# Where the later heads' values live, when they are loaded, and when the attention's output is written out

## The chip, the core and the metric

The kernel runs on one core of one Trainium2 chip. The metric is the device time of one execution in microseconds. Times of the kernel before are the median of three runs; the profile is one further execution, recorded by the hardware profiler.

## What is computed

Attention over 4 batches of 8 heads, with 32 global and 512 local positions of width 64 and a window of 32; its output is a matrix of 2176 rows and 512 columns, which goes through two MLPs without biases:

```python
out_g = np.matmul(sm(s_g), v_all)                 # global queries see every key
s_ll = np.where(mask, s_ll, -1000000000.0)        # local ones a window and the global keys
out_l = np.matmul(sm(np.concatenate([s_lg, s_ll], -1)), v_all)
x = np.concatenate([out_g, out_l], axis=2).transpose(0, 2, 1, 3).reshape(B * S, H * D)
h = np.maximum(x @ moe_w_in, 0.0)                 # d_ff 2048
x = h * h @ moe_w_out
h = (x @ moe2_w1) * (x @ moe2_w2) @ moe2_w3       # d_ff 1024
return h @ moe2_w_out
```

## The kernel before

Everything is float32 at the interface. Matrices of the MLPs, and keys, queries and values of the later heads, are split into a high and a low part that TensorE takes at full rate, and products are made of three passes (high by high, high by low, low by high).

The first part of the program, up to about 345 us, mixes attention with the first half of MLP 1. The loop `for i in range(0, NBLK, 2)` takes two blocks of rows (one batch's output, 256 and 288 columns) through the MLP in each turn. Its `main` list holds their matmul steps (`h_unit` with the weights ua, `x_unit_a` with ub); `merge` lays between them the attention `steps` of the next batch, b = i/2 + 1. So turn 0 carries batch 1, turn 2 batch 2 and turn 4 batch 3; turn 6 has no attention left and carries the conversions of further weights (`conv(16)` to `conv(32)`) instead. The steps come from `cycle(j)`: for a pair of heads, `emit_k` splits the keys and queries of the next pair (DVE L173 and L106) and moves them by five transfers per head (L179 to L183) into kq_hl; `emit_g` makes the global scores sg and pg (ACT L267, DVE L271 to L273), for which POOL copies global queries into qgp (L237); `emit_s` makes the local scores sc and softmax p (DVE L200, ACT L204, DVE L208 and L209, POOL L214); `emit_tg` and `emit_t` transpose pg and p into pt (tg L293, tp L305); `emit_pv` multiplies with the values and copies the result to xb (ACT L342, DVE L345 to L349).

Heads 0 to 15 use values in float32 (v_f). From head 16 (`FIRST_SPLIT`) on, `load_v` (L157) loads vraw and `emit_v` splits it into v_hl: a cast on DVE (L163) and a subtraction on POOL (L106); it then asks for the values two heads on. pt of these heads is a pair too, pt_hl.

Conversions take a weight matrix from DRAM (`load_w`, L409, into wraw) and turn it into a high and a low part: ACT L415 and L416, DVE L421 and L424, POOL L434, ACT L435, DVE L106.

Memory on chip is dealt out by pools that open and close like a stack on two sides. `cv` holds the conversions' buffers, `at` those of attention. At turn 2 both close, and `at2` (vraw and v_hl) and `sp` (pt_hl) take their places; at turn 6 the attention's pools close and `cv2` and `u2` open. What a new pool's tile lies on must have been read for the last time. `spill(i)` (L565) writes the attention's output of block i to DRAM (x_d), from where MLP 2's part fetches it again (`load_x`, L600); xb has two buffers, one for each batch in flight.

Each engine runs its instructions in one fixed order. That order is made when the program is built, by a scheduler that starts from the order of the code and moves instructions past each other. All transfers are issued from one queue, SP's, in its order.

Of the kernel before, what the change touches and what calls it, by code (L numbers as in the profile page):

```python
# [9 lines left out]
F32 = mybir.dt.float32  # L10
F32R = mybir.dt.float32r
# [9 lines left out]
B, H, SL, SG, D = 4, 8, 512, 32, 64  # L21
# [46 lines left out]
FIRST_SPLIT = 16  # L68
# [7 lines left out]
def attention_mlp(ctx: ExitStack, tc: tile.TileContext, kq0, kq, vw, wts, mask, ident, out):  # L76
    nc = tc.nc
# [3 lines left out]
    def pool(name, side="left", **kw):  # L81
        return tc.tile_pool(name=name, bufs=1, side=side, reuse_waits="tile", **kw)
# [3 lines left out]
    cv_cm, rot_cm, at_cm = pool("cv"), pool("rot", "right"), pool("at", "right")  # L86
    cv, rot, at = cv_cm.__enter__(), rot_cm.__enter__(), at_cm.__enter__()
# [12 lines left out]
    x_d = dram.tile([128, 4, NT], F32, name="x_d")  # L100
# [11 lines left out]
    pools = {"ua": sb, "ub": sb, "cv": cv}  # L112
# [9 lines left out]
    pair_t, kq_raw, kq_t, v_raw, v_t, p_t, pt_t = {}, {}, {}, {}, {}, {}, {}  # L122
# [25 lines left out]
    def load_v(i, part=None):  # L148

        if i >= (H if part is not None else B * H):  # L150
            return
        if i >= FIRST_SPLIT:
            t = v_raw[i] = at.tile([128, 8, D], F32, tag="vraw", name="vraw", bufs=2)
        else:
            t = v_t[i] = at.tile([128, 8, D], F32, tag="v", name="v_f32", bufs=3)
        c = slice(0, 8) if i >= H else slice(4, 8) if part == 0 else slice(0, 6)
        nc.sync.dma_start(out=t[:, c], in_=vw[i, :, c])  # L157

    def emit_v(i):
        if i >= FIRST_SPLIT:  # L160
            raw = v_raw.pop(i)
            t = v_t[i] = at.tile([128, 2, 8, D], F32R, tag="v", name="v_hl", bufs=2)
            nc.vector.tensor_copy(t[:, 0], raw)  # L163
            split_lo(nc.gpsimd, t[:, 1], raw, t[:, 0])
            load_v(i + 2)
# [109 lines left out]
    def new_pt(i):  # L275
        if i < FIRST_SPLIT:
            pt_t[i] = at.tile([128, 8, 160], F32, tag="pt", name="pt_f32", bufs=3)
        else:
            pt_t[i] = pools["cv"].tile([128, 2, 8, 160], F32R, tag="pt", name="pt_hl", bufs=2)

    def put_pt(i, to, src):

# [240 lines left out]
    def of(t, i):  # L523
        s, n = block(i)
        return t[:, :, s : s + n]
# [33 lines left out]
    def xcols(i):  # L559
        s, n = block(i)  # L560
        s -= S * (i // 2)
        return x_t[i // 2][:, :, s : s + n]

    def spill(i):
        nc.sync.dma_start(out=of(x_d, i), in_=xcols(i))  # L565

    steps = first_part()
    merge(steps, ([lambda n=n: conv(n) for n in range(8)], 0, len(steps) - 2))
# [7 lines left out]
    steps = [f for j in range(-1, 4) for f in cycle(j, ahead=j < 3)]  # L576
    main = [lambda f=f: h_unit(0, f, f) for f in range(8)]
# [18 lines left out]
    def load_x(i):  # L596

        if i < NBLK:
            t = x_t[i] = sb.tile([128, 2, 4, NB], F32, tag="xb", name="xl", bufs=2)[..., : block(i)[1]]
            nc.sync.dma_start(out=t[:, 0], in_=of(x_d, i))  # L600
            nc.sync.dma_start(out=t[:, 1], in_=of(part_d, i))

    for i in range(0, NBLK, 2):
        main = []
        for j in (i, i + 1):
            if j >= SHARED:
                main += rows(
                    j, 0, 8, lambda d, j=j: split_a(j + 1, d), lambda d, j=j: end_a(j, d, acc[d])
                )
                continue  # L610
            if j > 0:
                main += [lambda f=f, j=j: h_unit(j, f, f) for f in range(8)]
            main += [lambda d=d, j=j: x_unit_a(j, d) for d in range(4)]
        b = i // 2 + 1
        if b < B:
            if b == 1:
                spill(1)
                load_kq(H // 2)
                for k in range(H, min(H + 3, FIRST_SPLIT)):
                    load_v(k)  # L620
            if b * H == FIRST_SPLIT:
                at_cm.__exit__(None, None, None)
                cv_cm.__exit__(None, None, None)
                at_cm, cv_cm = pool("at2", "right"), pool("sp")
                at, pools["cv"] = at_cm.__enter__(), cv_cm.__enter__()
                for k in range(2):
                    load_v(FIRST_SPLIT + k)
            steps = [s for j in range(4 * b - 1, 4 * b + 4) for s in cycle(j, j < 4 * b + 3, j >= 4 * b)]
            steps.append(lambda i=i: (spill(i + 2), spill(i + 3)))
            fills = [(steps, 0, len(main) - 5)]  # L630
        else:
            for cm in (at_cm, rot_cm, cv_cm):
                cm.__exit__(None, None, None)
            u2 = pools["va"] = pools["vb"] = ctx.enter_context(pool("u2", "right"))
            pools["cv"] = ctx.enter_context(pool("cv2"))
            load_w(16)
            load_w(17)
            main.insert(18, lambda: load_x(0))
            fills = [([lambda n=n: conv(n) for n in range(16, 33)], 0, 31)]
        merge(main, *fills)  # L640

# [30 lines left out]
    main = []  # L672
# [146 lines left out]
```

## Time and profile before

| | |
|---|---|
| median of three runs | 945.86 us (944.57 to 948.61) |
| the profiled execution | 945.08 us, its span 943.3 us |
| PE busy | 899.1 us (95%) |
| DVE, ACT, POOL busy | 469.6, 499.5, 321.2 us |
| mean granted TensorE clock | 0.989 |

Busy time says how long an engine had an instruction running. The span is what the trace covers, from the first instruction to the last; the profiled execution's own time is 1.8 us more. The granted clock is a share of full speed: 1.0 is 2.4 GHz and 0.5 is 1.2 GHz. In the lists below, "PE" is TensorE, "PEld" its weight load, "SPq" the issue of a transfer on SP's queue. What stands in brackets at the end of a row is how long the engine was idle before it, and what let it go on.

### The profile page before, as it was taken

What the parts mean: (1) busy time and instruction counts of PE and PEld (TensorE: products, weight loads), DVE (VectorE), ACT (ScalarE), POOL (GpSimd) and SP (SyncE); (2) the same over time, 40 slices, a digit from 0 to 9 for tenths busy, and PEclk for the clock granted to TensorE, in tenths of its full rate; (3) what the DMA queues carried; (4) which work ended last, traced back from release to release, by engine and by line L of the source; (5) the groups of instructions that cost most, each with busy time, mean ns of one, the idle gap of its engine ahead of it and who ended that gap; (6) DMA issues with size and microseconds to landing.
All of it is one profiled execution on the core that took longest, in us unless ns stands there. A gap on an engine that the chain in (4) does not pass through costs nothing.

```text
span 943.3 us, 16424 instructions
## 1 busy us (share of the span) xinstructions
PE 899.1 (95%) x6064; PEld 822.3 (87%) x6064; DVE 469.6 (50%) x1139; ACT 499.5 (53%) x1291; POOL 321.2 (34%) x354
## 2 busy tenths in 40 slices
PE   7899899799999999988999999999999999999998
PEld 4677798699999989987999999999988888888886
DVE  6984465466867649999354353994110210200201
ACT  6975767657667748887464464884211211211211
POOL 5593452376656824433011121430211111111111
PEclk9999999989999999999999999999999999999999
DMA  8644667665668335656144333654200110100101
GB/s 269 204 148 115 168 156 186 184 142 127 156 188 200 84 108 172 227 178 202 32 157 146 132 112 134 207 192 133 98 23 1 43 42 1 42 1 1 42 1 42
DMA packets 61952, 113.07 MB, mean 120 GB/s; under 512 B 6320, under 2 KB 37168, under 8 KB 61872
## 3 DMA queue, kind: packets, MB, share of 16 engines
q1 hardware_dynamic: 61872, 112.03, 40.3%
q8 instruction: 48, 0.79, 0.3%
q14 instruction: 32, 0.26, 0.1%
HBM read 71.63 MB, written 19.92 MB: 97 GB/s over the span
## 4 chain that ended last, share of the span: by engine, by line
PE 63%; DMA 12%; DVE 10%; ACT 4%; issue 4%; POOL 4%; SPq 3%; DVEq 0%; POOLq 0%; ACTq 0%
PE ab L110 20%; PE acc L504 16%; PE h L110 9%; PE wacc L652 5%; PE x L110 4%; DMA wraw<-in_wts 4%; PE o L339 4%; DMA kq_hl<-kqhi 3%; PE sc L110 2%; DMA kqraw<-in_kq 2%; DVE wt L421 2%; DVE wt L424 2%; PE tp L305 2%; DVE hl L106 2%; POOL wt L434 1%
## 5 line engine op out<-in xcount | busy, mean ns | idle before, releaser
L434 POOL TENSOR_TENSOR wt<-wt 128x512 int32<-128x512 int32 x72 | 101.5, 1409 | 232.8 <-DVE wt L424 158.3
L723 DVE TENSOR_TENSOR r<-r,ab 128x480 f32<-128x480 f32 (+1 forms) x40 | 24.3, 607 | 220.2 <-PE ab L110 219.5
L110 PE MATMUL h<-hl,ua 128*128 128x256 f32 (+1 forms) x768 | 121.3, 303 | 8.5 <-ACT r L470 6.1
L110 PEld LDWEIGHTS h<-hl,ua 128*128 128x128 f32 x768 | 107.7, 200 | 12.4 <-ACT r L470 7.0
L504 PE MATMUL acc<-hl,vb 128*128 128x256 f32 (+1 forms) x768 | 112.9, 290 | 5.2 <-DVE hl L106 4.9
L110 PE MATMUL h<-hl,va 128*128 128x256 f32 (+1 forms) x768 | 112.3, 288 | 1.9 <-DVE hl L106 1.9
L106 POOL TENSOR_TENSOR hl_c<-r,hl_c 128x480 fp32r<-128x480 f32 x32 | 39.2, 1224 | 210.8 <-ACT hl_c L725 203.0
L504 PEld LDWEIGHTS acc<-hl,vb 128*128 128x128 f32 x768 | 103.0, 188 | 9.0 <-DVE hl L106 7.3
L110 PEld LDWEIGHTS h<-hl,va 128*128 128x128 f32 x768 | 102.9, 188 | 3.7 <-DVE hl L106 2.8
L110 PE MATMUL x<-hl,ub 128*128 128x288 f32 (+1 forms) x576 | 88.8, 295 | 3.3 <-POOL hl L106 3.3
L504 PE MATMUL acc<-hl_c,wv 128*128 128x480 f32 x384 | 89.2, 380 | 0.0
L110 PE MATMUL ab<-hl_c,ua 128*128 128x480 f32 x384 | 87.1, 380 | 0.0
L110 PE MATMUL ab<-hl_c,ub 128*128 128x480 f32 x384 | 86.6, 380 | 0.0
L110 PEld LDWEIGHTS ab<-hl_c,ub 128*128 128x128 f32 x384 | 72.0, 188 | 11.9
L722 ACT COPY r<-ab 128x480 f32<-128x480 f32 (+1 forms) x40 | 20.9, 522 | 116.1 <-PE ab L110 113.8
L110 PEld LDWEIGHTS ab<-hl_c,ua 128*128 128x128 f32 x384 | 71.9, 188 | 11.9
L110 PEld LDWEIGHTS x<-hl,ub 128*128 128x128 f32 x576 | 76.8, 189 | 6.1 <-POOL hl L106 4.5
L504 PEld LDWEIGHTS acc<-hl_c,wv 128*128 128x128 f32 x384 | 72.0, 188 | 11.4
L204 ACT ACTIVATE p<-p,st 128x256 f32<-128x256 f32 x128 | 64.2, 504 | 22.5 <-DVE st L200 22.3
L214 POOL TENSOR_TENSOR p<-p,st 128x512 f32<-128x512 f32 x56 | 61.8, 1106 | 35.4 <-DVE st L209 27.6
L470 ACT ACTIVATE r<-h 128x288 f32<-128x288 f32 (+1 forms) x128 | 49.2, 391 | 43.9 <-PE h L110 43.3
L415 ACT ACTIVATE wt<-wraw 128x512 f32<-128x512 f32 x72 | 48.4, 672 | 34.9 <-DMA wraw<-in_wts 32.4
(108 smaller groups left out, 1554.7 us busy)
## 6 DMA issues: line engine op xcount, KB each, us to landing
wraw<-in_wts SPq DMA_DIRECT2D x72, 512.0 KB, 3.4
kq_hl<-kqhi SPq DMA_DIRECT2D x24, 280.0 KB, 3.2
kq_hl<-kqraw SPq DMA_DIRECT2D x48, 136.0 KB, 3.2
vraw<-in_vw SPq DMA_DIRECT2D x16, 256.0 KB, 3.3
x2l<-x_d SPq DMA_DIRECT2D x4, 960.0 KB, 6.0
out<-y SPq DMA_DIRECT2D x16, 240.0 KB, 2.3
kqraw<-in_kq SPq DMA_DIRECT2D x24, 144.0 KB, 2.9
kq_hl<-kqraw SPq DMA_DIRECT2D x24, 144.0 KB, 3.4
```

Source lines behind the costliest of these rows:

```text
L106: eng.tensor_tensor(out=lo, in0=raw, in1=hi.bitcast(F32), op=ALU.subtract)
L110: mm(o, w, x, start=(k == 0), stop=(k == len(terms) - 1))
L204: nc.scalar.activation(p[:, n, :], p[:, n, :], AF.Exp, bias=least[:, n : n + 1], scale=-1.0, accum_out=sums[:, n, 0:1],)
L214: nc.gpsimd.tensor_tensor(out=p, in0=p, in1=over.unsqueeze(2).to_broadcast([128, 2, 256]), op=ALU.mult)
L339: mm(to, w, x, start=(k == 0), stop=(k == len(terms) - 1))
L415: nc.scalar.activation(t[0].bitcast(F32), raw[:, :, 1].bitcast(F32), AF.Copy, scale=2.0**-112)
L434: nc.gpsimd.tensor_tensor(out=b, in0=b, in1=m, op=ALU.add)
L470: nc.scalar.activation(r, h, AF.Relu)
L504: mm(acc[d], w[:, a, 128 * d : 128 * (d + 1)], g_t[f][:, b], start=(f + k == 0), stop=(f + k == 9),)
L652: mm(o, w3[:, a, 128 * q : 128 * (q + 1)], w_t[32 + 4 * half + q][:, b], start=(half + q + k == 0), stop=(half + q + k == 6),)
L722: nc.scalar.copy(r, a)
L723: nc.vector.tensor_tensor(out=r, in0=r, in1=b, op=ALU.mult)
```

## The change

Four things are different. At turn 0, as soon as the first 16 conversions are done, `cv` closes and `sp` opens on its memory; vraw and v_hl of the later heads lie in `sp`. At turn 2 `at` closes and `at2` opens; it now holds pt_hl. The first two loads of split values (heads 16 and 17) move from the start of turn 2 to the middle of the attention steps of turn 1's batch, that is of turn 0. The spills of a batch's output move from the end of the batch's own steps (block 1: from the start of turn 0) to the tenth place of the MLP steps of the next turn, and they are kept in program order: the scheduler doesn't move them.

```diff
--- before.py
+++ after.py
@@ -150,7 +150,7 @@
         if i >= (H if part is not None else B * H):
             return
         if i >= FIRST_SPLIT:
-            t = v_raw[i] = at.tile([128, 8, D], F32, tag="vraw", name="vraw", bufs=2)
+            t = v_raw[i] = pools["cv"].tile([128, 8, D], F32, tag="vraw", name="vraw", bufs=2)
         else:
             t = v_t[i] = at.tile([128, 8, D], F32, tag="v", name="v_f32", bufs=3)
         c = slice(0, 8) if i >= H else slice(4, 8) if part == 0 else slice(0, 6)
@@ -159,7 +159,7 @@
     def emit_v(i):
         if i >= FIRST_SPLIT:
             raw = v_raw.pop(i)
-            t = v_t[i] = at.tile([128, 2, 8, D], F32R, tag="v", name="v_hl", bufs=2)
+            t = v_t[i] = pools["cv"].tile([128, 2, 8, D], F32R, tag="v", name="v_hl", bufs=2)
             nc.vector.tensor_copy(t[:, 0], raw)
             split_lo(nc.gpsimd, t[:, 1], raw, t[:, 0])
             load_v(i + 2)
@@ -276,7 +276,7 @@
         if i < FIRST_SPLIT:
             pt_t[i] = at.tile([128, 8, 160], F32, tag="pt", name="pt_f32", bufs=3)
         else:
-            pt_t[i] = pools["cv"].tile([128, 2, 8, 160], F32R, tag="pt", name="pt_hl", bufs=2)
+            pt_t[i] = at.tile([128, 2, 8, 160], F32R, tag="pt", name="pt_hl", bufs=2)
 
     def put_pt(i, to, src):
 
@@ -562,7 +562,7 @@
         return x_t[i // 2][:, :, s : s + n]
 
     def spill(i):
-        nc.sync.dma_start(out=of(x_d, i), in_=xcols(i))
+        tc.keep_in_program_order(nc.sync.dma_start(out=of(x_d, i), in_=xcols(i)))
 
     steps = first_part()
     merge(steps, ([lambda n=n: conv(n) for n in range(8)], 0, len(steps) - 2))
@@ -614,19 +614,20 @@
         b = i // 2 + 1
         if b < B:
             if b == 1:
-                spill(1)
+                cv_cm.__exit__(None, None, None)
+                cv_cm = pool("sp")
+                pools["cv"] = cv_cm.__enter__()
                 load_kq(H // 2)
                 for k in range(H, min(H + 3, FIRST_SPLIT)):
                     load_v(k)
             if b * H == FIRST_SPLIT:
                 at_cm.__exit__(None, None, None)
-                cv_cm.__exit__(None, None, None)
-                at_cm, cv_cm = pool("at2", "right"), pool("sp")
-                at, pools["cv"] = at_cm.__enter__(), cv_cm.__enter__()
-                for k in range(2):
-                    load_v(FIRST_SPLIT + k)
+                at_cm = pool("at2", "right")
+                at = at_cm.__enter__()
             steps = [s for j in range(4 * b - 1, 4 * b + 4) for s in cycle(j, j < 4 * b + 3, j >= 4 * b)]
-            steps.append(lambda i=i: (spill(i + 2), spill(i + 3)))
+            if (b + 1) * H == FIRST_SPLIT:
+                steps.insert(len(steps) // 2, lambda: [load_v(FIRST_SPLIT + k) for k in range(2)])
+            main.insert(9, lambda i=i: spill(i + 1) if i == 0 else (spill(i), spill(i + 1)))
             fills = [(steps, 0, len(main) - 5)]
         else:
             for cm in (at_cm, rot_cm, cv_cm):
@@ -635,7 +636,8 @@
             pools["cv"] = ctx.enter_context(pool("cv2"))
             load_w(16)
             load_w(17)
-            main.insert(18, lambda: load_x(0))
+            main.insert(9, lambda i=i: (spill(i), spill(i + 1)))
+            main.insert(19, lambda: load_x(0))
             fills = [([lambda n=n: conv(n) for n in range(16, 33)], 0, 31)]
         merge(main, *fills)
```

What the scheduler makes of it is seen on three engines. The first place is SP's queue at the boundary between batch 1 and batch 2; kqraw are the raw keys and queries of pair 9, kq_hl their split parts (first five transfers: head 18). Brackets name what is waited for. Before:

```order
L146 DMA kqraw<-in_kq 64x576 [waits DMAHW3_49]
L179 DMA kq_hl<-kqhi 64x1120 [waits DVE_49,DMAHW4_49,PE_49,Pool_49]
L180 DMA kq_hl<-kqhi 64x544 [waits DMAHW5_49]
L181 DMA kq_hl<-kqraw 64x576 [waits DMAHW6_49,DMAHW0_49,DVE_49]
L565 DMA x_d<-xb 512x1x256 [waits DMAHW7_49,Activation_49]
L157 DMA vraw<-in_vw 128x512
L157 DMA vraw<-in_vw 128x512 [waits DMAHW1_49,PE_49]
L565 DMA x_d<-xb 512x1x288 [waits DMAHW2_49,DVE_49]
L182 DMA kq_hl<-kqraw 64x544 [waits DMAHW3_49]
L183 DMA kq_hl<-kqraw 64x544 [waits DMAHW4_49]
L179 DMA kq_hl<-kqhi 64x1120 [waits DMAHW5_49,PE_49,Pool_49]
```

After:

```order
L146 DMA kqraw<-in_kq 64x576 [waits DMAHW6_49]
L565 DMA x_d<-xb 512x1x288 [waits DMAHW7_49]
L179 DMA kq_hl<-kqhi 64x1120 [waits DVE_49,DMAHW0_49,PE_49,Pool_49]
L180 DMA kq_hl<-kqhi 64x544 [waits DMAHW1_49]
L181 DMA kq_hl<-kqraw 64x576 [waits DMAHW3_49,DMAHW2_49,DVE_49]
L182 DMA kq_hl<-kqraw 64x544
L183 DMA kq_hl<-kqraw 64x544 [waits DMAHW4_49]
L179 DMA kq_hl<-kqhi 64x1120 [waits DMAHW5_49,PE_49,Pool_49]
```

The spill of block 1 (512x1x288) now stands between the last load of keys and the first move; the two loads of vraw, and the spills of blocks 2 and 3 (512x1x256 and 512x1x288), no longer stand between the moves L181 and L182.

The second place is VectorE at the same boundary, in the softmax of heads 16 and 17 (st_82 to st_85) and the global scores of that pair (stg_86). Before:

```order
L163 CAST v_hl<-vraw 128x512
L208 TENSOR_REDUCE st_82<-st_82 128x2
L163 CAST v_hl<-vraw 128x512
L209 RECIPROCAL st_82<-st_82 128x2
...
L208 TENSOR_REDUCE st_83<-st_83 128x2
L209 RECIPROCAL st_83<-st_83 128x2
L271 TENSOR_REDUCE stg_86<-stg_86 64x1
L272 RECIPROCAL stg_86<-stg_86 64x1
L273 TENSOR_SCALAR pg<-pg,stg_86 64x640
```

After:

```order
L208 TENSOR_REDUCE st_82<-st_82 128x2
L209 RECIPROCAL st_82<-st_82 128x2
...
L208 TENSOR_REDUCE st_83<-st_83 128x2
L209 RECIPROCAL st_83<-st_83 128x2
L271 TENSOR_REDUCE stg_86<-stg_86 64x1
L272 RECIPROCAL stg_86<-stg_86 64x1
L273 TENSOR_SCALAR pg<-pg,stg_86 64x640
```

The two casts L163 are gone from here; they stand where L271 to L273 of pair 3's global scores are (77 us in the trace before), one cast between L271 and L272, one behind L273.

The third place is ACT at the start of turn 6, behind the last copies of the attention's output. Before:

```order
L342 COPY xb<-o 64x256
L460 CAST hl<-xb 128x256
L342 COPY xb<-o 64x256
L582 COPY st<-x 128x288
L415 ACTIVATE wt<-wraw 128x512
L416 ACTIVATE wt<-wraw 128x512
L470 ACTIVATE r<-h 128x256
L415 ACTIVATE wt<-wraw 128x512
```

After:

```order
L342 COPY xb<-o 64x256
L460 CAST hl<-xb 128x256
L342 COPY xb<-o 64x256
L415 ACTIVATE wt<-wraw 128x512
L416 ACTIVATE wt<-wraw 128x512
L582 COPY st<-x 128x288
L470 ACTIVATE r<-h 128x256
L415 ACTIVATE wt<-wraw 128x512
L416 ACTIVATE wt<-wraw 128x512
```

The first conversion, L415 and L416, now stands ahead of the copy L582 and of the relu L470. On SP the loads of these weights (L409) waited before for the last products with values, with the spill of block 6 ahead of them and that of block 7 behind; after, the first waits for POOL's split of head 31's values, and both spills stand behind five further loads.

On TensorE, 36 h matmuls follow the transposes tg of pair 8 before; after, they are followed by two matmuls of sg for the next pair, four transposes tp and 12 h matmuls. On POOL, the cast L237 that needs the last moves (L182, L183) of head 18 stands after ahead of L473 and L106 of the MLP, and before behind them.

## Rows read from the trace of the kernel before

**Rows 1.** Windows by stage: us, PE, PEld, DVE, ACT, POOL busy (x count), PEclk, DMA share, GB/s.
```profile
170.00:200.00 30.00, 22.87 (x151) 21.75 (x151) 14.18 (x46) 13.80 (x45) 16.32 (x23) 0.83 0.70 181
200.00:345.00 145.00, 143.79 (x1316) 141.44 (x1315) 101.42 (x355) 99.36 (x312) 93.44 (x118) 1.00 0.54 135
345.00:440.00 95.00, 84.31 (x636) 81.20 (x635) 84.26 (x123) 75.27 (x175) 35.83 (x26) 0.98 0.59 195
```

**Rows 2.** Waits in 170 to 200 us: us in total, times, longest.
```profile
PE tg L293 <- DVE st L208: 4.7, 1, 4.7
...
PE o L339 <- DVE xb L347: 1.9, 1, 1.9
```

**Rows 3.** Timeline of the first boundary: start us, us, engine, line, operation [idle before <-releaser].
```profile
177.64 0.21 POOL L237 CAST qgp<-kq_hl 128x32 fp32r<-128x32 f32 x1 [9.84 <-DMA kq_hl<-kqhi]
...
179.47 0.61 POOL L473 TENSOR_TENSOR r<-r 128x256 f32<-128x256 f32 x1 [1.62 <-ACT hl L471]
...
180.16 0.74 POOL L106 TENSOR_TENSOR hl<-r,hl 128x256 fp32r<-128x256 f32 x1
...
181.98 0.20 ACT L267 ACTIVATION_READ_ACCUMULATOR pg<-pg,stg 64x1 f32 x1
...
182.23 1.11 PE L110 MATMUL x<-hl,ub 128*128 128x256 f32 x8
...
183.15 0.43 DVE L163 CAST v_hl<-vraw 128x512 fp32r<-128x512 f32 x1 [2.86 <-DMA vraw<-in_vw]
...
186.13 0.13 DVE L271 TENSOR_REDUCE stg<-stg 64x1 f32<-64x3 f32 x1
...
186.49 1.40 DVE L273 TENSOR_SCALAR pg<-pg,stg 64x640 f32<-64x640 f32 x1
186.51 1.04 POOL L214 TENSOR_TENSOR p<-p,st 128x512 f32<-128x512 f32 x1
```

**Rows 4.** All of line L273: count, min/median/max ns, first and last start.
```profile
L273 DVE TENSOR_SCALAR pg<-pg,stg x16: 534/546/1402, 48.5 to 321.6; 64x640 f32<-64x640 f32 x16
```

**Rows 5.** Timeline of SP's issues at the first boundary.
```profile
173.70 0.49 SPq L179 DMA_DIRECT2D kq_hl<-kqhi  x1
...
175.72 0.65 SPq L565 DMA_DIRECT2D x_d<-xb  x1
...
176.42 2.13 SPq L157 DMA_DIRECT2D vraw<-in_vw  x2
...
179.26 0.63 SPq L182 DMA_DIRECT2D kq_hl<-kqraw  x1
```

**Rows 6.** Timeline of PE before and after the stop, same shape.
```profile
180.81 1.57 PE L110 MATMUL h<-hl,ua 128*128 128x256 f32 x12
...
188.73 7.17 PE L110 MATMUL h<-hl,ua 128*128 128x256 f32 x36
```

**Rows 7.** Windows around the stops of the first boundary, columns as in the first group.
```profile
174.10:177.60 3.50, 3.50 (x17) 3.17 (x16) 2.12 (x9) 1.12 (x3) 0.00 (x0) 0.51 0.81 159
...
187.80:194.60 6.80, 6.57 (x32) 6.48 (x33) 1.39 (x8) 1.78 (x6) 5.83 (x10) 0.50 0.55 161
```

**Rows 8.** Timeline of the second boundary.
```profile
344.83 0.36 ACT L342 COPY xb<-o 64x256 f32<-64x256 f32 x1
...
350.96 0.66 ACT L415 ACTIVATE wt<-wraw 128x512 f32<-128x512 f32 x1 [2.63 <-DMA wraw<-in_wts]
...
352.50 0.73 PE L110 MATMUL h<-hl,ua 128*128 128x256 f32 x4 [2.13 <-ACT r L470]
```

**Rows 9.** DMA issues of the whole span: count, KB each, median us from issue to landing.
```profile
wraw<-in_wts SPq DMA_DIRECT2D x72, 512.0 KB, 3.4
...
x_d<-xb SPq DMA_DIRECT2D x4, 576.0 KB, 6.1
```

**Rows 10.** Lines of DVE, 200 to 345 us: busy, mean ns, idle before.
```profile
L163 DVE CAST v_hl<-vraw 128x512 fp32r<-128x512 f32 x14 | 8.3, 593 | 2.0 <-PE o L339 1.1 <-issue 0.4 <-POOL qgp L237 0.3
```

**Rows 11.** Timeline in the first batches, POOL.
```profile
82.60 1.04 POOL L214 TENSOR_TENSOR p<-p,st 128x512 f32<-128x512 f32 x1 [4.85 <-DVE st L209]
```

## The prediction

> **What bounds the kernel now.** I read first the table of stretches [rows 1]. It shows a kernel that is TensorE almost throughout: PE is busy 143.79 of 145 us while batches 2 and 3 run. Two stretches leak. At the boundary from batch 1 to batch 2 (170 to 200 us) PE works 22.87 of 30 us and its mean clock is 0.83; in 345 to 440 us, where attention has ended and the second run of conversions starts, it works 84.31 of 95. What the change can win lies in these 7.1 and 10.7 us of idle time and in the low clock; elsewhere it can only cost.
>
> Next I read who ends the waits there. At the first boundary one wait is most of the stretch: 4.7 us in front of the transposes tg of pair 8 [rows 2]. The reader should follow it backwards in the timeline [rows 3]. PE's x matmuls end at 182.23 + 1.11 = 183.34, then comes nothing until tg. tg needs pg scaled by L273, and L273 starts only at 186.49, although ACT's last read of the sums, on which L271 to L273 depend, ends at 181.98 + 0.20 = 182.18. Between stands VectorE's own order: the cast L163 of head 16's values, which waited 2.86 us for vraw, a second cast, and the softmax sums behind them. vraw is late because its two loads were issued at 176.42 [rows 5], between other transfers: at2 and sp, which hold it, open only at this boundary.
>
> At the second boundary [rows 8] ACT's last copy of the attention ends at 344.83 + 0.36 = 345.19, and the first conversion L415 starts at 350.96, after a wait for the first weights, whose load stands on SP behind the last PV and beside the last spills. L470, which releases the next MLP chain, is behind it in ACT's order, so PE has a wait of 2.13 at 352.50.
>
> **The change, part by part.** The profiled execution took 945.08 us, its span 943.3; the sum is made against 945.08, and 945.86 (the median) is 0.78 more.
>
> *The stall before tg.* The order after has no L163 between L200 and L273 of pair 8. L271 to L273 can then follow ACT's 182.18. From L271's start to L273's are 186.49 − 186.13 = 0.36, and L273 itself has a median of 0.546 [rows 4]: 182.18 + 0.36 + 0.55 = 183.1, before PE's 183.34. So all of 4.7 can go. But L273 took 1.40 here, while POOL's L214 ran from 186.51 [rows 3]. If it meets POOL again, it ends at 182.18 + 0.36 + 1.40 = 183.94, 0.6 after PE. The bounds are −4.7 and −4.1; I take −4.4. The Trainium skill, page "SBUF — State Buffer", section "Who interferes with whom", has the rule for it: VectorE and GpSimd share one pair of ports as an exclusive lock, and a tensor_scalar in its fast mode and a GpSimd instruction can hold each other up. The rows agree (1.40 against 0.546); by the rule this term is −4.1 if POOL works at 182.5, −4.7 if it rests.
>
> *The clock.* After the stall the granted clock is 0.50 from 187.80 to 194.60 [rows 7], the lower of the two levels (1.2 GHz), and 36 h matmuls take 7.17 us, while 12 of the same shape took 1.57 just before the stall [rows 6]: 36 at that rate are 4.71. If PE doesn't stand still, 7.17 − 4.71 = 2.46 is won. Below nothing is excluded, since those matmuls can't run slower than at the lower level. Bounds −2.5 and 0; I take −2.5: the lower level follows PE's stops, here the one of 4.7 us, and in 174.10 to 177.60 (0.51) one of 1.9 us [rows 2, 7].
>
> *Spill(1) just ahead of the keys.* The order moves the 576 KB write of block 1 from batch 1's first third to a place in front of L179 at 173.70 [rows 5], and takes vraw and the spills of 2 and 3 from between L181 and L182. The second is the gain that makes room: L182 can start where the spill stood, 175.72, instead of at 179.26, so SP is 3.5 us ahead. The first costs: the write shares the engines with the loads of the next keys and with the kq_hl moves. It landed 6.1 us after its issue in the median [rows 9]; a kq_hl move landed after 177.64 − 173.70 = 3.9 [rows 3, 5]. If the moves behind the spill lose the difference, 2.2, this is the price; nothing, if they share. I take +0.6. The Trainium skill, page "DMA: Bandwidth & Descriptors", section "Issuing engines are not separate DMA queues", says that all transfers run on the same 16 engines and interleave; by it the spill isn't served whole before the next move, and the price stays below 2.2. No row isolates this.
>
> *POOL's new order.* After, the second qgp cast of head 18 stands ahead of L473 and L106 (before at 179.47 and 180.16, ending at 180.90). It needs L183, now issued about 0.65 behind 175.72, so landed at 176.4 + 3.9 = 180.3, cast by 180.5: L106 then ends near 182.0, and the x matmuls which read it run from 182.23. Zero, with 0.2 in hand; it costs the spill's 2.2 once more if that cover is gone, which is the first rival.
>
> *The values loaded early.* Two loads, two casts and two splits stand now near 70 to 82 us, one cast between L271 and L272 of an earlier pair. A cast is 0.593 [rows 10]; POOL waits 4.85 before 82.60 there [rows 11], which hides two splits, each about the price of L214 here (1.04). One cast delays tg of that pair by at most 0.6. I take +0.2 (0 to 0.9).
>
> *The other spills.* Those of blocks 2 to 5 go to the middle of the steps of batches 2 and 3, where MLP matmuls hide what keys and values wait for: PE stands idle 145 − 143.79 = 1.2 us in all there [rows 1]. Zero, and 6.1 − 3.4 = 2.7 each [rows 9] if a weight or key load had to pay for it. Those of 6 and 7 go behind five weight loads: L565 no longer shares the engines with the first two, but with later ones. +0.5 (0 to 2.7).
>
> *The start of the conversions.* The order has vraw's memory, not pt's, under the new weights: the first load waits for POOL's split of head 31 and no longer for the last PV, and L415 follows L342 directly. At best L415 starts at 345.19 instead of 350.96: −5.8. At the least PE's wait of 2.13 goes, since L470 is no longer behind a wait for a load [rows 8]. The whole stretch follows the conversions' pace, but the second L415 stays behind L470; I take the middle, −4.0.
>
> Sum: −4.4 − 2.5 + 0.6 + 0.2 + 0.5 − 4.0 = −9.6, so 935.5 for an execution like the profiled one, and 936.3 beside the median. I forecast **936.3**.
>
> **The rivals.** *A: another wait takes the stall's place.* The keys of head 18 come behind the spill, POOL stands on its qgp cast, L106 and L214 behind it are late, and PE, which after tg now goes straight to sg and tp instead of 36 h matmuls, waits for them. L273 meets POOL, the spill costs its whole 2.2, and a stop of this size keeps the clock down: −4.1 (stall) + 0 (clock) + 2.2 (spill) + 0.2 + 0.5 − 4.0 = −5.2, so 939.9 for the profiled execution and 940.7 beside the median. For it: the margin of 0.2 above. Against it: the DMA queue is relieved of two vraw loads and two spills at that very place.
>
> *B: the clock falls all the same.* The sum without the 2.5 is −7.1: 938.8. For it: a stop of 1.9 us was enough at 173, and that stop isn't touched. Against it: 345 to 440 us has 10.7 us of idle time in short pieces and a mean of 0.98 [rows 1].
>
> *C: earlier weights are of no use at the second boundary,* because DVE and ACT are the conversions' bound and PE waits elsewhere for the same work: −4.0 becomes 0, 940.3. Against it: PE's 2.13 at 352.50 has a named cause.
>
> *D: slower.* The other 14 casts move in VectorE's order too, and later ones stand now with a wait for PE between L271 and L272. If each holds up softmax and so PE, the 9.6 gain and 4.7 (0.5%) more are gone at (9.6 + 4.7) / 14 = 1.02 us of PE idle per cast: 950.6 and up. For it: the order. Against it: the casts are 0.593 and their 14 together waited 2.0 us [rows 10].
>
> *E: it doesn't do what it says:* the loads land no sooner. The order excludes this; 945.9 at a small chance.
>
> **How the numbers follow.** 0.5% of 945.86 is 4.7, about what a measurement of this kernel can tell from no change: faster ends at 941.1, slower begins at 950.6. Chances: forecast 0.46, B 0.19, A 0.15, C 0.12, D 0.05, E 0.03. A and C lie less than 1 us inside the bound, so I count some of each, 0.12 together, beyond it: faster is 0.46 + 0.19 + 0.27 − 0.12 = 0.80, slower 0.05, the same 0.12 + 0.03 = 0.15. The best bounds of all terms give −4.7 − 2.5 + 0 + 0 + 0 − 5.8 = −13.0, 932.9, and some of the idle 10.7 us beyond could follow: low 931. The range goes up to A's and C's 940.7 with a little more: high 942.
>
> **What would show it.** Right: no wait of 4.7 before tg near 183; no stretch at half clock behind it; no wait of VectorE for vraw; L182 right behind L181 on SP; L415 at about 345.3; PE's idle time in the 95 us behind batch 3 down from 10.7 to about 7. Wrong: a wait for kq_hl, qgp or tp behind tg; L106 of POOL ending after 183; the conversions' later waits (PE for hl) growing by what the start gains; VectorE's casts with a wait for PE in front of sums that PE needs.

## The result, and the profile after

The changed kernel took 935.27 us in the median of four runs (932.75 to 936.63); the kernel before took 945.23 beside them. The ratio is 0.9876, with an interval of 0.985 to 0.9903. The profiled execution has a span of 932.6 us, 10.7 less than before. The windows by stage, columns as in [rows 1]:

```profile
170.00:200.00 30.00, 27.22 (x212) 26.03 (x211) 17.21 (x64) 19.48 (x65) 16.62 (x26) 0.89 0.57 136
200.00:345.00 145.00, 143.57 (x1300) 141.09 (x1300) 99.45 (x340) 97.55 (x299) 91.36 (x114) 1.00 0.58 149
345.00:440.00 95.00, 89.20 (x690) 86.35 (x689) 87.24 (x131) 80.84 (x188) 38.63 (x28) 1.00 0.63 209
```

Compared with [rows 1], PE's idle time falls from 7.1 to 2.8 us in 170 to 200 us and from 10.7 to 5.8 in 345 to 440; in between nothing changes. But the first of these rows flatters: the changed kernel has a new stop just ahead of 170. The waits of PE in 165 to 200 us (us in total, times, longest):

```profile
PE tp L305 <- POOL p L214: 2.6, 1, 2.6
...
PE x L110 <- POOL hl L106: 2.5, 1, 2.5
```

The waits of [rows 2] are both gone, tg's 4.7 us and the 1.9 us for xb. In their place stand two others of almost the same length as each other, both for POOL. Counted over 165 to 200 us, PE's idle time went from 7.1 to 5.4 us, and the clock's loss (35 us times what the mean lacks to 1) from 0.15 × 35 = 5.3 to 0.10 × 35 = 3.5: 12.4 before, 8.9 after. The timeline shows what happens in place of [rows 3]:

```profile
176.82 0.70 SPq L183 DMA_DIRECT2D kq_hl<-kqraw  x1
...
181.47 0.55 DVE L273 TENSOR_SCALAR pg<-pg,stg 64x640 f32<-64x640 f32 x1
...
182.39 0.21 POOL L237 CAST qgp<-kq_hl 128x32 fp32r<-128x32 f32 x1 [4.13 <-DMA kq_hl<-kqraw]
182.56 0.61 POOL L473 TENSOR_TENSOR r<-r 128x256 f32<-128x256 f32 x1
...
183.25 0.72 POOL L106 TENSOR_TENSOR hl<-r,hl 128x256 fp32r<-128x256 f32 x1
...
184.03 1.65 PE L110 MATMUL x<-hl,ub 128*128 128x256 f32 x6 [2.54 <-POOL hl L106]
```

VectorE is in time: L273 ends at 182.02, 4.5 us earlier than it started before, and took 0.55, not 1.40. Now POOL is late. Its cast of head 18's query waits for the last key move (L183), issued at 176.82; it runs at 182.39, 5.6 us later. L473 and L106 of the MLP stand behind it, and PE's x matmuls, which read what L106 writes, wait 2.54 us until 184.03. Behind this stop the clock is at its lower level again:

```profile
184.00:191.00 7.00, 6.97 (x34) 6.63 (x35) 2.63 (x5) 1.71 (x5) 7.00 (x10) 0.52 0.31 82
```

The second boundary is as the order let expect; these rows answer to [rows 8]:

```profile
330.10 6.03 SPq L409 DMA_DIRECT2D wraw<-in_wts  x2
...
341.83 0.37 ACT L342 COPY xb<-o 64x256 f32<-64x256 f32 x1
...
342.23 0.66 ACT L415 ACTIVATE wt<-wraw 128x512 f32<-128x512 f32 x1
...
345.70 0.39 ACT L470 ACTIVATE r<-h 128x256 f32<-128x256 f32 x1 [0.54 <-PE h L110]
```

The first two weight loads are issued from 330.10 on (6.03 us for both issues, since SP waits between them), so the weights lie there when ACT is done with attention, and L415 starts 0.03 us behind the last L342 (341.83 + 0.37 = 342.20). Before it was 5.77. L470 follows at 345.70, and PE's wait of 2.13 us is gone.

### The profile page after: what moved, and what is told of

The parts are those of the page before. It is cut to its first block, busy times and chain, and to the rows that moved or that the text cites. A ratio compares the mean times of both kernels' runs of the same rounds, so it can differ in the third digit from the quotient of the medians.

```text
span 932.6 us, 16416 instructions
## 1 busy us (share of the span) xinstructions
PE 895.3 (96%) x6064; PEld 818.9 (88%) x6064; DVE 468.8 (50%) x1139; ACT 501.6 (54%) x1291; POOL 322.3 (35%) x354
## 4 chain that ended last, share of the span: by engine, by line
PE 68%; DMA 11%; ACT 7%; DVE 6%; issue 3%; POOL 2%; SPq 1%; DVEq 0%; ACTq 0%; POOLq 0%
PE ab L110 20%; PE acc L504 17%; PE h L110 11%; PE x L110 6%; DMA wraw<-in_wts 6%; PE wacc L654 5%; PE o L339 4%; PE sc L110 2%; PE tp L305 2%; DMA kq_hl<-kqhi 2%; ACT wt L415 1%; DMA wl<-w_d 1%; DVE hl L106 1%; ACT p L204 1%; ACT wt L416 1%
## 5 line engine op out<-in xcount | busy, mean ns | idle before, releaser
L110 PEld LDWEIGHTS h<-hl,ua 128*128 128x128 f32 x768 | 105.2, 195 | 10.1 <-ACT r L470 4.8
L106 POOL TENSOR_TENSOR hl_c<-r,hl_c 128x480 fp32r<-128x480 f32 x32 | 39.2, 1224 | 210.8 <-ACT hl_c L727 210.8
L214 POOL TENSOR_TENSOR p<-p,st 128x512 f32<-128x512 f32 x56 | 61.1, 1096 | 33.6 <-DVE st L209 31.2
L470 ACT ACTIVATE r<-h 128x288 f32<-128x288 f32 (+1 forms) x128 | 49.2, 392 | 39.1 <-PE h L110 37.3
L727 ACT CAST hl_c<-r 128x480 fp32r<-128x480 f32 x32 | 19.0, 593 | 84.3 <-DVE r L725 84.3
```

What stands on the lines that cost most here:

```text
L106: eng.tensor_tensor(out=lo, in0=raw, in1=hi.bitcast(F32), op=ALU.subtract)
L110: mm(o, w, x, start=(k == 0), stop=(k == len(terms) - 1))
L214: nc.gpsimd.tensor_tensor(out=p, in0=p, in1=over.unsqueeze(2).to_broadcast([128, 2, 256]), op=ALU.mult)
L470: nc.scalar.activation(r, h, AF.Relu)
L727: nc.scalar.copy(g[:, 0], r)
```

## The experiments

Each was timed in several rounds beside the kernel before on the same chip. "First boundary" is PE's idle time in 165 to 200 us plus what the clock's mean lacks in it (its two decimals make that 0.35 us coarse); "second" is PE's idle time in the 95 us behind the last L342; the next column is the gap from that L342's end to the first L415; all from the one profiled execution of each kernel, which for two of them (spill 1 old, spills 6 and 7 old) was the slowest of those timed.

| kernel | median, before beside it | ratio, interval | first boundary | second | gap |
|---|---|---|---|---|---|
| before | 945.23 | | 7.1 + 5.3 | 10.7 | 5.8 |
| changed | 935.27, 945.23 | 0.9876, 0.985 to 0.9903 | 5.4 + 3.5 | 5.8 | 0.0 |
| changed, again | 931.91, 944.74 | 0.9861, 0.9842 to 0.9879 | 3.1 + 1.8 | 5.3 | 0.0 |
| spills only | 940.45, 946.95 | 0.9929, 0.9902 to 0.9955 | 4.7 + 1.8 | 7.9 | 1.1 |
| memory only | 938.8, 946.95 | 0.9912, 0.9885 to 0.994 | 4.4 + 1.8 | 8.2 | 5.7 |
| changed, spill 1 old | 935.67, 946.95 | 0.9876, 0.9841 to 0.9911 | 4.4 + 1.8 | 6.0 | 0.0 |
| changed, late loads | 937.7, 946.95 | 0.9901, 0.9872 to 0.993 | 3.5 + 3.5 | 8.2 | 1.1 |
| changed, spills 6 and 7 old | 938.15, 944.74 | 0.9924, 0.9901 to 0.9947 | 4.7 + 3.5 | 7.1 | 5.9 |
| spills 2 and 3 only | 941.3, 945.08 | 0.9961, 0.9945 to 0.9978 | 5.2 + 1.8 | 9.8 | 5.8 |
| spills 6 and 7 only | 939.43, 945.08 | 0.9937, 0.9917 to 0.9957 | 4.9 + 7.0 | 8.0 | 0.0 |

**The spills alone.** The kernel before with the spills, and nothing else, moved:

```diff
-        nc.sync.dma_start(out=of(x_d, i), in_=xcols(i))
+        tc.keep_in_program_order(nc.sync.dma_start(out=of(x_d, i), in_=xcols(i)))
...
-                spill(1)
...
-            steps.append(lambda i=i: (spill(i + 2), spill(i + 3)))
+            main.insert(9, lambda i=i: spill(i + 1) if i == 0 else (spill(i), spill(i + 1)))
...
-            main.insert(18, lambda: load_x(0))
+            main.insert(9, lambda i=i: (spill(i), spill(i + 1)))
+            main.insert(19, lambda: load_x(0))
```

> Only the spills are moved; values and pools stay as in the kernel before. My theory: the casts of the values still stand in front of the sums of pair 8, so a stop of 3 to 5 us before tg stays, and the first weights still wait for the last products, so L415 still starts some 5 us behind the last L342: 942 to 945 us, a gain of at most 3. Rival 1, that the moved spills alone bring the gain of the second boundary: L415 follows L342 at once and the time is 936 to 939.

Measured: 940.45, a ratio of 0.9929. My forecast fell on both counts. There is no stop before tg, although both casts stand in VectorE's order where they stood, and L415 starts 1.1 us behind the last L342. But VectorE is still late: L271 starts at 186.47, 1.14 us behind ACT's last read of the sums (before: 3.95), and L273 ends at 188.42, 1.1 us behind PE's x matmuls. PE doesn't wait since the scheduler has also laid 12 h matmuls (1.57 us) between x and tg, where tg stood right behind x before. PE's longest waits in 165 to 200 us:

```profile
PE tp L305 <- POOL p L214: 2.2, 1, 2.2
PE sc L110 <- DVE pt_hl L106: 1.7, 1, 1.7
PE x L110 <- POOL hl L106: 0.5, 1, 0.5
```

**The memory alone.** Three lines: split values from the pool `sp`, pt from `at2`, both opened at turn 2 as before, loads and spills where they stood.

```diff
-            t = v_raw[i] = at.tile([128, 8, D], F32, tag="vraw", name="vraw", bufs=2)
+            t = v_raw[i] = pools["cv"].tile([128, 8, D], F32, tag="vraw", name="vraw", bufs=2)
-            t = v_t[i] = at.tile([128, 2, 8, D], F32R, tag="v", name="v_hl", bufs=2)
+            t = v_t[i] = pools["cv"].tile([128, 2, 8, D], F32R, tag="v", name="v_hl", bufs=2)
-            pt_t[i] = pools["cv"].tile([128, 2, 8, 160], F32R, tag="pt", name="pt_hl", bufs=2)
+            pt_t[i] = at.tile([128, 2, 8, 160], F32R, tag="pt", name="pt_hl", bufs=2)
```

> Only the memory is exchanged: split values in sp, pt in at2, both opened at turn 2 as in the kernel before, loads and spills left where they stand in the code. The scheduler itself puts the first four loads of values near 70 us. My theory: the stop before tg loses its cast, but the spills of blocks 2 and 3 stay between the key moves, so a stop of 2 to 4 us stays there; the first weights wait for POOL instead of PE but stand behind the spill of block 6; 939 to 942. Rival 2, that the memory alone is the change's gain: 935 to 937. If the place of the loads in the code mattered, nothing would be gained at the first boundary: 943 or more.

Measured: 938.8, 0.9912. The first two loads went to 71.39 us by themselves: the memory of the conversions is free by then, and the scheduler needs no line of code to tell it. The stop before tg is gone here too, although the spills still stand between the key moves, and here nothing hides a late VectorE: tg stands right behind x as before, and L271 starts 0.03 us behind ACT's last read.

```profile
177.37 0.80 SPq L182 DMA_DIRECT2D kq_hl<-kqraw  x1
178.26 1.71 SPq L565 DMA_DIRECT2D x_d<-xb  x1
...
183.51 0.15 DVE L271 TENSOR_REDUCE stg<-stg 64x1 f32<-64x3 f32 x1
183.51 1.10 PE L110 MATMUL x<-hl,ub 128*128 128x256 f32 x8
...
184.58 0.49 PE L293 MATMUL tg<-ident_sb,pg 64*128 64x64 f32 x5
```

So the stop is absent with either half of the change alone. The gains are 0.71% and 0.88%, together 1.24% to 1.39%; that is less than their sum, but within the intervals. By the table it is the first boundary where they don't add (6.5 and 6.2 us are left with one half, 8.9 and 4.9 in the two profiles with both). At the second boundary the load stands behind a spill, as expected:

```profile
343.69 0.56 SPq L565 DMA_DIRECT2D x_d<-xb  x1
...
344.42 1.49 SPq L409 DMA_DIRECT2D wraw<-in_wts  x2
...
347.46 0.85 ACT L470 ACTIVATE r<-h 128x256 f32<-128x256 f32 x2 [2.02 <-PE h L110]
...
350.20 0.67 ACT L415 ACTIVATE wt<-wraw 128x512 f32<-128x512 f32 x1 [1.58 <-DMA wraw<-in_wts]
```

The first L415 is as late as before. But here ACT's order has two L470 ahead of it, and PE has no wait of 2 us for it.

**The changed kernel with block 1's spill at its old place.**

```diff
-        tc.keep_in_program_order(nc.sync.dma_start(out=of(x_d, i), in_=xcols(i)))
+        d = nc.sync.dma_start(out=of(x_d, i), in_=xcols(i))
+        if i > 1:
+            tc.keep_in_program_order(d)
...
+                spill(1)
                 load_kq(H // 2)
...
-            main.insert(9, lambda i=i: spill(i + 1) if i == 0 else (spill(i), spill(i + 1)))
+            if i > 0:
+                main.insert(9, lambda i=i: (spill(i), spill(i + 1)))
```

> The changed kernel with the spill of block 1 back at the start of turn 0; all else as changed. My theory: the stop of 2.5 us before the x matmuls (POOL on the cast of head 18's query, which waits for the last key move) comes from that spill's 576 KB ahead of the key moves; without it the stop falls under 1 us and the time is 932 to 934, 1 to 3 less than the changed kernel's 935.3. Rival, that the key moves take this long by themselves: the stop stays at 2 to 3 us and the time within 1 us of 935.

Measured: 935.67 and the changed kernel's ratio, 0.9876. The rival holds. No spill is near, and POOL's cast still runs 5.2 us after L183's issue, and PE waits 2.03:

```profile
180.90 0.70 SPq L183 DMA_DIRECT2D kq_hl<-kqraw  x1
...
186.13 0.36 POOL L237 CAST qgp<-kq_hl 128x32 fp32r<-128x32 f32 x1 [3.80 <-DMA kq_hl<-kqraw]
...
187.92 0.98 PE L110 MATMUL x<-hl,ub 128*128 128x256 f32 x6 [2.03 <-POOL hl L106]
```

What changes with the place of this spill is which of two stops of 2 us comes ahead of the x matmuls. In every kernel of the table with the spill of block 1 at the boundary, PE waits 2.1 to 2.6 us for POOL ahead of tp; in the others 1.8 to 2.2 us for xb ahead of o.

**The changed kernel with late loads.** The first two loads of values are put back to the start of turn 2. Without a further line the scheduler takes them forward again, and its order on VectorE and POOL is the changed kernel's own; so they were held there.

```diff
+        d = nc.sync.dma_start(out=t[:, c], in_=vw[i, :, c])
+        if i in (FIRST_SPLIT, FIRST_SPLIT + 1):
+            tc.keep_in_program_order(d)
...
                 at = at_cm.__enter__()
+                for k in range(2):
+                    load_v(FIRST_SPLIT + k)
-            if (b + 1) * H == FIRST_SPLIT:
-                steps.insert(len(steps) // 2, lambda: [load_v(FIRST_SPLIT + k) for k in range(2)])
```

> The changed kernel with the first two loads of split values held at the boundary (start of turn 2, order kept), in the new memory. My theory: VectorE waits for them again in front of the sums of pair 8, a stop of 3 to 5 us before tg and the lower clock behind it are back, the second boundary keeps its gain: 937 to 940. Rival, that the first boundary gives nothing because another wait takes the stop's place: within 1 us of 935.

Measured: 937.7, 0.9901. The time is in the range, for another reason than I gave: no stop before tg came back. The loads land 3.2 and 3.4 us after their issue, L271 (line 273 in this kernel) starts 0.85 us behind ACT's last read, and 12 h matmuls stand between x and tg here too, so that what is left of VectorE's delay costs PE nothing. What it gives up against the changed kernel is at the second boundary, 8.2 us of idle time in place of 5.3 to 5.8.

**The changed kernel again,** unchanged, beside the next three kernels on one chip.

> The changed kernel once more, unchanged, on the same chip as the three others of this call, so that differences of 2 to 4 us between them can be read: 933 to 937 us, a stop of 2 to 3 us before the x matmuls at the first boundary and half clock behind it.

Measured: 931.91, 0.9861, below what I expected, and the profiled execution has no stop at x:

```profile
168.39 1.11 PE L305 MATMUL tp<-ident_sb,p 128*128 128x128 f32 x4 [2.31 <-POOL p L214]
...
177.03 0.69 SPq L183 DMA_DIRECT2D kq_hl<-kqraw  x1
...
180.58 0.21 POOL L237 CAST qgp<-kq_hl 128x32 fp32r<-128x32 f32 x1 [2.12 <-DMA kq_hl<-kqraw]
...
181.44 0.74 POOL L106 TENSOR_TENSOR hl<-r,hl 128x256 fp32r<-128x256 f32 x1
...
182.72 1.04 POOL L214 TENSOR_TENSOR p<-p,st 128x512 f32<-128x512 f32 x1
...
182.97 1.14 DVE L273 TENSOR_SCALAR pg<-pg,stg 64x640 f32<-64x640 f32 x1
...
184.25 0.49 PE L293 MATMUL tg<-ident_sb,pg 64*128 64x64 f32 x5 [0.56 <-DVE st L208]
```

L183 is issued at 177.03 and POOL's cast runs at 180.58, 3.6 us later, where it was 5.6 in the first profile of the same program. L106 ends at 182.18 and PE waits 0.56 us, before tg: L273 met POOL's L214 here and took 1.14 us, not 0.55. The windows show the clock: the lower level stands behind the stop of 2.31 us at 168, and 184 to 191 us is at full speed.

```profile
168.40:171.00 2.60, 2.60 (x11) 2.30 (x12) 0.00 (x0) 1.39 (x3) 1.09 (x2) 0.50 0.49 134
...
184.00:191.00 7.00, 6.75 (x58) 6.71 (x59) 3.84 (x10) 5.37 (x17) 7.00 (x10) 1.00 0.34 92
```

So the new stop is not in every execution. What differs ahead of it is what was in flight beside L183: the first move of the next head (L179, 280 KB) followed it by 0.81 us in the first profile and by 2.03 in the second. In the three other kernels with 5.2 to 5.5 us from issue to use it followed by 0.8 to 1.1. But with the spills alone it followed by 0.6, and L183 landed in 3.9; so this cause isn't shown.

**The changed kernel with the spills of blocks 6 and 7 at their old place.**

```diff
+        if i < 6:
+            tc.keep_in_program_order(d)
...
+            if i == 4:
+                steps.append(lambda: (spill(6), spill(7)))
             fills = [(steps, 0, len(main) - 5)]
...
-            main.insert(9, lambda i=i: (spill(i), spill(i + 1)))
-            main.insert(19, lambda: load_x(0))
+            main.insert(18, lambda: load_x(0))
```

> The changed kernel with the spills of blocks 6 and 7 back at the end of batch 3's steps. The load of the first weights stands again behind the spill of block 6. If early weights bring the gain of the second boundary, L415 starts again 5 us behind the last L342, PE's idle time from there to 440 us is 10 us as before, and the time 4 to 6 us above the changed kernel. If it is ACT's order that brings it (L470 stands ahead of L415 here), the idle time is 7 to 9 us and the time 1 to 3 above the changed kernel.

Measured: 938.15, 6.2 us over the changed kernel beside it, with a wide spread (933.94 to 941.36). The load is behind the spill again, and L415 starts 5.9 us behind the last L342:

```profile
345.01 0.56 SPq L565 DMA_DIRECT2D x_d<-xb  x1
...
345.68 1.55 SPq L409 DMA_DIRECT2D wraw<-in_wts  x2
...
349.38 0.38 ACT L470 ACTIVATE r<-h 128x256 f32<-128x256 f32 x1 [0.60 <-PE h L110]
351.67 0.66 ACT L415 ACTIVATE wt<-wraw 128x512 f32<-128x512 f32 x1 [1.91 <-DMA wraw<-in_wts]
```

Yet PE's idle time behind it is only 7.1 us, since L470 at 349.38 runs ahead of L415. The time speaks for the early weights, the idle time for ACT's order. The profiled execution (941.36) also lost time far from these two spills: its clock has a mean of 0.93 in the first 82 us, 0.96 and 0.98 in the changed kernel's two profiles, and at the first boundary it has the stop at x (2.43 us, POOL's cast 5.5 us behind L183's issue), in all 8.2 us there against the 4.9 of the kernel beside it. So what these two spills cost lies somewhere between the 1.8 us of idle time and the 6.2 of the medians; the runs don't settle it.

**Query casts elsewhere.** Three kernels tried to keep the MLP's L473 and L106 from standing behind the cast: held on POOL behind the work traced before (pair 9), the casts of pair 9 on ACT, and held for pairs 8 and 9.

```diff
-                    nc.gpsimd.tensor_copy(q[:, c : c + SG], x[:, :SG])
+                    d = nc.gpsimd.tensor_copy(q[:, c : c + SG], x[:, :SG])
+                    if j == 9:
+                        tc.keep_in_program_order(d)
```

```diff
-                    nc.gpsimd.tensor_copy(q[:, c : c + SG], x[:, :SG])
+                    (nc.scalar.copy if j == 9 else nc.gpsimd.tensor_copy)(q[:, c : c + SG], x[:, :SG])
```

> The changed kernel with the four query casts of pair 9 held on POOL behind the work traced before them, so that L473 and L106 of the MLP no longer stand behind a wait for the last key move of head 18. If that order is the cause of the new stop, the stop of 2.5 us before the x matmuls and the 7 us at half clock behind it go: 929 to 933 us, 3 to 6 under the changed kernel. Rival: tg or sg waits in its place, within 1.5 us of the changed kernel.

> The changed kernel with the four query casts of pair 9 on ACT in place of POOL. POOL is free of the wait for the key move, but ACT's cast of head 18 now stands ahead of the exponentials of pair 8 and of L267. If a wait at the head of an engine's queue is the mechanism, the stop moves from the x matmuls to tg, 2 to 3 us, and the time stays within 2 us of the changed kernel. If only POOL's slowness were the cause, the stop is gone: 930 to 933.

> The changed kernel with the query casts of pairs 8 and 9 held on POOL behind the work traced before them. In the changed kernel L214 of head 15 stands behind the cast of head 17's query, which waits for a key move, and PE stops 2.3 to 2.6 us before tp at 168 us. If that order is the cause, this stop and the half clock near it go: 1 to 4 us under the changed kernel's 932 to 935, so 929 to 933. Rival: sg of pair 8 now waits for the casts, 934 to 938.

Measured: 933.36 (0.987, 0.9851 to 0.9889), 934.52 (0.9884, 0.9863 to 0.9904) and 933.37 beside 945.08 (0.9881, 0.9858 to 0.9905). None differs from the changed kernel by more than the intervals. None of the three profiles has a stop at x. In the second the wait is before tg, as expected, but it is 0.6 us and not 2 to 3. The changed kernel's own profile beside them had no stop at x to move, so as tests of it they are inconclusive. In the third the stop before tp is gone as well, and PE waits 2.8 us for VectorE before an h matmul instead: one stop against another, with no gain that the medians show.

**The spills of blocks 2 and 3 alone,** in the kernel before:

```diff
+        if i in (2, 3):
+            tc.keep_in_program_order(d)
...
+            if i == 2:
+                main.insert(9, lambda: (spill(2), spill(3)))
+            if i > 0:
+                steps.append(lambda i=i: (spill(i + 2), spill(i + 3)))
-            steps.append(lambda i=i: (spill(i + 2), spill(i + 3)))
```

> The kernel before with one thing changed: the spills of blocks 2 and 3 go nine steps into the next batch. Values, pools and all other spills as before. If the stop of 4.7 us came from the loads of values sharing the engines with these two writes, the loads land 3.5 to 4 us after their issue instead of 6.7, the stop and the half clock behind it are gone although both casts still stand in VectorE's order ahead of the sums: 938 to 942 us. If the place of the casts is enough for the stop, it stays at 3 to 5 us: 944 or more.

Measured: 941.3, 0.9961. The loads of values stand where they stood, at the boundary:

```profile
176.96 1.40 SPq L157 DMA_DIRECT2D vraw<-in_vw  x2
...
178.40 0.48 SPq L183 DMA_DIRECT2D kq_hl<-kqraw  x1
...
180.43 0.52 DVE L163 CAST v_hl<-vraw 128x512 fp32r<-128x512 f32 x1 [0.31 <-DMA vraw<-in_vw]
...
183.47 0.43 DVE L163 CAST v_hl<-vraw 128x512 fp32r<-128x512 f32 x1 [1.79 <-DMA vraw<-in_vw]
183.79 0.21 POOL L237 CAST qgp<-kq_hl 128x32 fp32r<-128x32 f32 x1 [3.13 <-issue]
183.96 1.27 POOL L106 TENSOR_TENSOR v_hl<-vraw,v_hl 128x512 fp32r<-128x512 f32 x1
...
184.90 0.13 DVE L271 TENSOR_REDUCE stg<-stg 64x1 f32<-64x3 f32 x1
...
185.96 0.98 PE L110 MATMUL x<-hl,ub 128*128 128x256 f32 x6 [2.78 <-POOL hl L106]
...
186.78 1.56 PE L110 MATMUL h<-hl,ua 128*128 128x256 f32 x12
...
188.27 0.52 PE L293 MATMUL tg<-ident_sb,pg 64*128 64x64 f32 x5
```

The first, issued at 176.96, lets VectorE cast at 180.43, 3.5 us later; before it was 6.7, from 176.42 to 183.15 [rows 3, 5]. The second landed 5.7 us after its issue, 7.1 before. There is no wait before tg. But that doesn't make the two writes (1088 KB together) the cause of the old stop: L271 still starts 2.15 us behind ACT's last read (182.56 + 0.19 = 182.75), and what hides it is a stop at x of 2.78 us and 12 h matmuls that now stand between x and tg. The stop at x comes from POOL: its cast waits for L183 (issued at 178.40) until 183.79, and behind it the split of head 16's values, 1.27 us, stands ahead of the L106 that x needs.

**The spills of blocks 6 and 7 alone,** in the kernel before:

```diff
+        if i in (6, 7):
+            tc.keep_in_program_order(d)
...
+            if i < 4:
+                steps.append(lambda i=i: (spill(i + 2), spill(i + 3)))
-            steps.append(lambda i=i: (spill(i + 2), spill(i + 3)))
...
-            main.insert(18, lambda: load_x(0))
+            main.insert(9, lambda: (spill(6), spill(7)))
+            main.insert(19, lambda: load_x(0))
```

> The kernel before with only the spills of blocks 6 and 7 moved, behind the first weight loads. The first boundary stays as before, 4.7 us stop and half clock included. If the weights' early start is the gain of the second boundary, L415 follows the last L342 within 2 us, the wait of PE for L470 of 2.1 us is gone and the time is 939 to 942. If the memory under the weights (values in place of pt) is needed for it, 943 to 945.

Measured: 939.43, 0.9937, in the range. The first boundary, where the order is the kernel before's, keeps its stops, tg's shorter in this execution. The loads of values, beside the same two writes, landed 4.9 and 5.5 us after their issue (before: 6.7 and 7.1), and L271 starts 1.94 us behind ACT's last read:

```profile
PE tg L293 <- DVE st L208: 2.3, 1, 2.3
PE o L339 <- DVE xb L347: 2.1, 1, 2.1
```

At the second the weights are asked for 5 us earlier and L415 follows the last L342 at once, in the old memory:

```profile
339.80 1.26 SPq L409 DMA_DIRECT2D wraw<-in_wts  x2
...
344.59 0.36 ACT L342 COPY xb<-o 64x256 f32<-64x256 f32 x1
344.98 0.67 ACT L415 ACTIVATE wt<-wraw 128x512 f32<-128x512 f32 x1
```

## Why the prediction was right

I forecast 936.3 (931 to 942); 935.27 and 931.91 were measured. Both gains were where I put them, but that the sum came so close is luck: in the first profile the first boundary gave 2.8 us less than my terms for it, and the second 2.8 us more.

*The stall before tg* (−4.4): gone in the first profile; in the second 0.56 us of it are left. In the first L273 didn't meet POOL and took 0.55 us. In the second it took 1.14 beside L214 and ended 0.42 us behind PE's x matmuls, so that 4.7 − 0.56 = 4.1 were won, the lower of my two bounds. The rule of the Trainium skill, page "SBUF — State Buffer", section "Who interferes with whom", and the trace agree there, as they do in the spills-only kernel, where L273 took 1.60 us beside POOL's L106 of 186.78. The cause that I gave, VectorE's casts waiting for vraw in front of the sums, is borne out by the memory alone: the two writes stay, the casts go, and with tg still right behind x the stop is gone. How much of vraw's lateness was the writes is open. Without them the first load landed in 3.2 to 3.6 us and the second in 3.4 to 5.7; beside them it was 6.7 and 7.1 in one profile, 4.9 and 5.5 in another of the same order.

*POOL's new order* (zero, 0.2 in hand): this step failed. I took 3.9 us from issue to use for L183, from one row of another move (L179); it was 5.6 in the first profile and 3.6 in the second, and 5.2 to 5.5 in three other kernels. With 5.6 the wait of rival A comes true: L106 ends at 183.97, and PE waits 2.54 us. A margin of 0.2 us on a transfer that varies by 2 is no margin.

*The clock* (−2.5): it hangs on the same stop. In the first profile 7 us stay at the lower level (rival B), in the second 2.6 us do. First boundary in all: 3.5 us won in the first profile and 7.5 in the second; my terms for it, stall, clock and spill, made 6.3. Which of the two is the usual case the two profiles can't say.

*Spill(1)* (+0.6): nothing that shows, a ratio of 0.9876 with it and without, each with about 0.3% to either side. The waits ahead of it changed names, 1.9 us for xb into 2.3 to 2.6 for POOL. The rule of the Trainium skill that I cited (page "DMA: Bandwidth & Descriptors", section "Issuing engines are not separate DMA queues") is in line with the other spills: vraw's loads took 4.9 to 7.1 us beside two writes and 3.2 to 5.7 without.

*The values loaded early* (+0.2): PE's idle time in the first 82 us is 14.6 us before and 14.7 after (15.0 in the second profile). *The other spills* (+0.5): no wait of PE names them; moving all of them, as the spills-only kernel does, gains.

*The start of the conversions* (−4.0): mis-sized. L415 starts right behind L342, as I said, and PE's idle time fell by 4.9 us instead of about 4, and the mean clock of the stretch rose from 0.98 to 1.00, which is 1.9 us more: −6.8. It takes both halves of the change. Spills or memory alone leave 7.9 to 8.2 us of the 10.7; 5.3 to 6.0 are left only with both. That isn't enough by itself: with late loads, which have both halves, 8.2 are left. The wait of 2.13 for L470 explains the first step: either the weights are early, or L470 stands ahead of L415. The rest lies in later waits for VectorE's splits (2.1 and 1.6 us in the spills-only kernel at 392 and 429, none over 1.0 in the changed one); that they come from how the scheduler lays the splits between the conversions is argued, not shown.

Rivals C, D and E didn't come. With the other casts in their new places PE's idle time in 200 to 345 us is 1.4 and 1.9 us, 1.2 before, and every part tried alone was a gain.

## What to carry to other kernels

When a wait names a late load, look at what stands behind the load in the waiting engine's order, and at what else moves in the same microseconds. And when a wait is gone, check that the instruction it waited for has really become earlier: here moving the loads brought VectorE in time, while moving the writes beside them left it 1.1 to 2.2 us late, and the wait was gone since other work had come to stand in front of it. With a scheduler like this one a tile's memory decided how early its load went (71 us, from a line at turn 2) and the line's place in the code did not; to hold a transfer back it has to be pinned. After a stop is removed, ask which engine has a waiting instruction at its head next, and price that wait with the range of the transfer's times, not with one of them.

## What the runs showed that I had not expected

The same program, profiled twice, had the same key move in use 3.6 and 5.6 us after its issue; with it a stop of 2.5 us and some 4 us more at the lower clock came or stayed away, and the medians of the two sets of runs were 935.27 and 931.91. A stop of 1.9 to 2.6 us was enough, in several profiles, for the lower clock behind it; not every such stop had one. The old stop varied too: with the same order at the first boundary, tg waited 4.7 us in one profile and 2.3 in another.
